# Block transposes that write with stride four, whole-tile loads and stores, and a new hand-written order in a hashed-attention and MLP kernel

## The chip, the cores and the metric

The kernel runs on one core of a Trainium2 chip. The metric is device time in microseconds (us) of one execution. Five engines work from queues of their own: PE (TensorE, matrix products), DVE (VectorE), ACT (ScalarE), POOL (GpSimd) and SP (SyncE, which here only issues transfers). An instruction starts when it is at the head of its engine's queue and what it waits for is there.

## The reference, cut to what matters

Attention in which a query sees only keys with the same six-bit hash, then a layer norm and a two-layer MLP with a residual.

```python
q_bits = (np.einsum('bhsd,dk->bhsk', q, proj) > 0)      # k_bits likewise; 6 bits
mask = q_bucket[:, :, :, None] == k_bucket[:, :, None, :]
scores = np.where(mask, scale * np.matmul(q, k.transpose(0, 1, 3, 2)), -1e9)
attn = softmax(scores); x = np.matmul(attn, v)           # 4 batches, 8 heads, 768 rows, 64 wide
x = x.transpose(0, 2, 1, 3).reshape(4, 768, 512)
xn = (x - mu) / np.sqrt(var + 1e-06) * g_ln
out = x + np.maximum(xn @ w_ch1, 0.0) @ w_ch2            # 512 -> 2048 -> 512
```

## The kernel before

The work is cut into 12 units u: batch b = u // 3 and a third of its 768 queries, 256 rows. A unit has six score steps s = 6u ... 6u+5, three key blocks of 256 for each of two groups g of four heads.

**A score step.** `S` is 24 matmuls (L476): hash signs from `G` and two halves of q and k, summed so that equal hashes lift a score. It writes two PSUM pairs, heads 0 and 1 into `sc(s, 0)`, heads 2 and 3 into `sc(s, 1)`. `E` (L482, ACT) takes the exponential of one pair, 128x1024, and frees it. `A` (L501) multiplies E by the values `vaug` into `acc`. The pairs have the tags scA and scB; only for the steps in `ROT = (2, 1, 0)`, the first three, a third pair, `acc`, takes part in turn.

**After three steps of a group:** `na`, `nb` normalize (L514, L521, L523), `nc` and `ce` are the statistics and centring (L527, L530, L531), `rs` is on POOL. `fl` transposes the result by a DMA into `xnT`; unit 0 does it by PE (`ft`, `fc`). `F.u.p` (L558, 8 matmuls) is the first MLP product for two of 16 hidden blocks, `R` its relu on DVE or ACT, `D` the second product (L574), `Z` the residual (L582), `O` the store (L592).

**The feed.** A tile `X` holds q or k as loaded, 32 sequence rows on the partitions of each head. DVE transposes 32x32 blocks (`turn`, L234): `tn` for batch 0 in pieces of one key block (`tp`, 128x256, two instructions per piece), `tu` for later batches (`T`, 128x384, eight per group). The sequence index is 32-row block, `c` (0..3) and `t` (0..31) mixed: a transpose writes contiguously, so that within each 128 columns the order is (c, t) and not the natural (t, c). Batch 0 puts its keys right in the casts and hash copies (`ca`, `bh`, `bi`, through `key_order`); later batches instead load the values in four 32-partition pieces (`lv`, L378), and every output is stored in four such pieces (L592). The hash signs come through `ha` (L323) and `bh`, or for the rest of batch 0 through `hc`, `bc`, `sl`, `bi` (L334 to L359), later through `hm`, `bt` and a DRAM round trip `mw`, `mr`. `cv` casts values on POOL, `su`, `sp`, `sq`, `sc` sum them. `lw1`, `lw2` are the weight loads, issued by POOL; `wm` and `warm` are matmuls on ones while the first loads are under way, and `wa`, the same into unused columns of `acc`, is defined but not in the order.

**What sets the order.** A list of words written into the source, each an operation, its engine (t PE, v DVE, a ACT, p POOL, s SP) and its arguments. The kernel issues them in that sequence, so each engine's queue order is the list's.

Of the kernel before, what the change touches and what calls it, by code (L numbers as in the profile page):

```python
# [13 lines left out]
NWARM = 8  # L14

ROT = (2, 1, 0)
# [3 lines left out]
on.p.0 mem.v lp.a tab.a warm.t wm.t.0 wm.t.1 lx.s.0.0.0.1 lx.s.0.1.1.3 pf.v wm.t.2 wm.t.3 lx.s.1.1.0.3 lx.s.0.1.0.1  # L20
lx.s.1.0.0.1 tn.v.0.0.0 ca.a.0.0.0 lx.s.1.0.1.3 lv.s.0.0.4 lv.s.0.4.4 sel.p lx.s.0.0.1.3 p32.p ha.t.0.0.0 wm.t.4 wm.t.5
tn.v.0.1.2 ca.a.0.1.2 bh.v.0.0.0 tn.v.0.1.1 ca.p.0.1.1 ha.t.0.1.2 ha.t.0.1.1 bh.v.0.1.2 S.t.2.2 tn.v.1.1.2 ca.p.1.1.2
wm.t.6 wm.t.7 E.a.2.0 E.a.2.1 lg.s tn.v.0.1.0 ha.t.0.1.0 bh.v.0.1.1 tn.v.1.0.0 S.t.1.2 E.a.1.0 ca.p.0.1.0 ca.p.1.0.0
bh.v.0.1.0 tn.v.1.1.1 ca.v.1.1.1 ha.t.1.1.1 cv.p.0.0.0 E.a.1.1 gx.p.1.0.0 LX.s.1.0.0 bh.v.1.1.1 cv.p.0.0.2 S.t.0.2
E.a.0.0 ha.t.1.0.0 tn.v.1.1.0 ha.t.1.1.0 bh.v.1.0.0 S.t.4.2 bh.v.1.1.0 E.a.0.1 ca.p.1.1.0 tn.v.1.0.2 ha.t.1.1.2
bh.v.1.1.2 cv.p.0.4.2 tn.v.0.0.2 lv.s.1.4.3 A.t.1.2 cv.p.0.4.0 E.a.4.0 sq.t.0.0 lw1.p.2 E.a.4.1 lv.s.1.0.3 S.t.3.2
A.t.2.2 lv.s.1.4.0 sc.a.0.0 lw1.p.1 E.a.3.0 tn.v.0.0.1 hc.t.0.0.2 hc.t.0.0.1 bc.v.0.0.1 E.a.3.1 bc.v.0.0.2 sl.t.0.0.1
bi.a.0.0.1 ca.v.0.0.1 tn.v.1.0.1 sl.t.0.0.2 S.t.5.2 ca.p.1.0.1 lv.s.1.4.1 bi.a.0.0.2 E.a.5.0 A.t.0.2 na.v.0.0 nb.v.0.0
nc.v.0.0 sq.t.0.4 E.a.5.1 sc.v.0.4 S.t.8.2 gx.v.1.0.1 E.a.8.0 gx.v.1.1.0 A.t.5.2 A.t.4.2 ca.p.1.0.2 tu.v.1.0.0.0
LX.s.1.0.1 A.t.3.2 E.a.8.1 na.v.0.1 nb.v.0.1 lw1.p.3 S.t.6.2 E.a.6.0 lv.s.1.0.1 nc.v.0.1 ce.v.0.0 hc.t.1.0.2 hc.t.1.0.1  # L30
A.t.8.2 bc.v.1.0.1 E.a.6.1 S.t.7.2 A.t.6.2 bc.v.1.0.2 lv.s.1.4.2 ce.v.0.1 E.a.7.0 pmem.p tu.v.1.0.0.1 rs.p.0 gx.v.1.1.1
sl.t.1.0.1 on.p.1 sl.t.1.0.2 LX.s.1.1.1 bi.v.1.0.2 bi.v.1.0.1 E.a.7.1 lw1.p.0 tu.v.1.0.0.3 ft.t.0.1 ft.t.0.0 fc.v.0.0
LX.s.1.1.0 S.t.9.2 tu.v.1.0.1.2 fc.a.0.1 A.t.7.2 lw2.p.1 lw2.p.0 tu.v.1.0.1.1 lw2.p.3 ca.a.0.0.2 cv.p.1.4.0 F.t.0.4
tu.v.1.0.1.3 E.a.9.0 E.a.9.1 na.v.1.0 F.t.0.3 R.v.0.4 S.t.10.2 R.a.0.3 A.t.9.2 lw2.p.2 E.a.10.1 F.t.0.6 tu.v.1.0.0.2
CA.v.1.0.0 E.a.10.0 nb.v.1.0 nc.v.1.0 R.a.0.6 F.t.0.7 S.t.11.2 E.a.11.0 tu.v.1.0.1.0 E.a.11.1 CA.p.1.0.1 su.p.1.4
hm.t.1.0 bt.v.1.0 A.t.10.2 R.a.0.7 tu.v.1.1.0.2 tu.v.1.1.1.3 tu.v.1.1.1.1 S.t.14.2 tu.v.1.1.0.1 mw.s.1.0 mr.s.1.0.0
F.t.0.2 tu.v.1.1.0.3 R.v.0.2 A.t.11.2 E.a.14.1 na.v.1.1 nb.v.1.1 E.a.14.0 F.t.0.5 tu.v.1.1.1.2 S.t.12.2 R.v.0.5 F.t.0.0
E.a.12.0 nc.v.1.1 R.v.0.0 E.a.12.1 A.t.14.2 F.t.0.1 S.t.13.2 A.t.12.2 R.a.0.1 lv.s.1.0.2 D.t.0.0.0 E.a.13.0 ce.v.1.0
E.a.13.1 D.t.0.0.1 ce.v.1.1 rs.p.1 fl.s.1.1 tu.v.1.1.1.0 fl.s.1.0 tu.v.1.1.0.0 mr.s.1.0.3 S.t.16.2 E.a.16.0 E.a.16.1
LX.s.2.0.0 mr.s.1.0.2 hm.t.1.1 lv.s.1.0.0 bt.v.1.1 CA.p.1.1.0 mr.s.1.0.1 D.t.0.0.2 mw.s.1.1 sp.t.1.4 sc.v.1.4 S.t.15.2  # L40
cv.p.1.4.2 F.t.1.7 R.v.1.7 E.a.15.0 E.a.15.1 cv.p.1.0.0 A.t.13.2 D.t.0.0.3 na.v.2.0 F.t.1.5 CA.a.1.1.1 Z.v.0.0 S.t.17.2
LX.s.2.1.1 E.a.17.1 R.v.1.5 mr.s.1.1.3 su.p.1.0 D.t.0.1.0 F.t.1.2 R.v.1.2 LX.s.2.0.1 mr.s.1.1.1 mr.s.1.1.0 LX.s.3.0.1
D.t.0.1.1 E.a.17.0 S.t.18.2 E.a.18.1 lv.s.2.0.3 mr.s.1.1.2 F.t.1.3 R.v.1.3 D.t.0.1.2 D.t.0.1.3 nb.v.2.0 E.a.18.0
F.t.1.0 lv.s.2.0.0 A.t.15.2 S.t.20.2 E.a.20.0 R.v.1.0 F.t.1.1 R.a.1.1 Z.v.0.1 tu.v.2.0.0.1 A.t.17.2 nc.v.2.0 A.t.16.2
F.t.1.4 cv.p.1.0.2 tu.v.2.0.0.3 E.a.20.1 S.t.19.2 E.a.19.0 na.v.2.1 A.t.20.2 R.v.1.4 nb.v.2.1 nc.v.2.1 ce.v.2.1
lv.s.2.4.1 tu.v.2.0.0.2 D.t.1.0.0 E.a.19.1 fl.s.2.1 F.t.1.6 R.a.1.6 S.t.21.2 D.t.1.0.1 E.a.21.0 E.a.21.1 lv.s.2.4.2
ce.v.2.0 tu.v.2.0.0.0 D.t.1.0.2 D.t.1.0.3 CA.p.2.0.0 tu.v.2.0.1.0 tu.v.2.0.1.1 sp.t.1.0 sc.a.1.0 A.t.18.2 fl.s.2.0
S.t.22.2 E.a.22.1 LX.s.2.1.0 E.a.22.0 tu.v.2.0.1.2 tu.v.2.0.1.3 CA.a.2.0.1 hm.t.2.0 O.s.0.0 lv.s.2.0.1 Z.v.1.0 bt.v.2.0
D.t.1.1.0 S.t.23.2 F.t.2.0 LX.s.3.0.0 E.a.23.1 D.t.1.1.1 lv.s.2.4.3 lv.s.2.4.0 R.a.2.0 E.a.23.0 tu.v.2.1.0.0 lv.s.2.0.2
A.t.19.2 na.v.3.0 F.t.2.5 R.a.2.5 cv.p.2.4.0 S.t.24.2 E.a.24.0 D.t.1.1.2 tu.v.2.1.1.2 F.t.2.3 su.p.2.0 E.a.24.1 R.v.2.3  # L50
rs.p.2 A.t.23.2 S.t.26.2 F.t.2.2 D.t.1.1.3 nb.v.3.0 tu.v.2.1.1.1 cv.p.2.0.0 E.a.26.1 E.a.26.0 R.v.2.2 A.t.21.2 F.t.2.1
R.a.2.1 O.s.0.3 tu.v.2.1.0.1 S.t.25.2 nc.v.3.0 Z.v.1.1 mw.s.2.0 E.a.25.0 O.s.0.2 O.s.1.3 E.a.25.1 A.t.22.2 na.v.3.1
nb.v.3.1 F.t.2.4 tu.v.2.1.1.0 O.s.0.1 mr.s.2.0.2 D.t.2.0.0 tu.v.2.1.1.3 R.a.2.4 S.t.29.2 sp.t.2.0 sc.v.2.0 A.t.25.2
E.a.29.0 A.t.26.2 tu.v.2.1.0.3 O.s.1.0 F.t.2.7 cv.p.2.0.2 nc.v.3.1 ce.v.3.1 E.a.29.1 R.a.2.7 S.t.28.2 A.t.24.2 F.t.2.6
E.a.28.0 lv.s.3.4.2 LX.s.3.1.0 E.a.28.1 cv.p.2.4.2 D.t.2.0.1 ce.v.3.0 R.a.2.6 tu.v.2.1.0.2 S.t.31.2 fl.s.3.1 E.a.31.0
fl.s.3.0 E.a.31.1 CA.p.2.1.1 hm.t.2.1 bt.v.2.1 tu.v.3.0.1.0 tu.v.3.0.1.2 mw.s.2.1 mr.s.2.1.0 mr.s.2.1.2 D.t.2.0.2
rs.p.3 tu.v.3.0.1.3 mr.s.2.1.3 S.t.27.2 su.p.2.4 E.a.27.0 D.t.2.0.3 na.v.4.0 F.t.3.7 A.t.28.2 R.v.3.7 E.a.27.1 S.t.30.2
E.a.30.0 lv.s.3.0.1 Z.v.2.0 A.t.27.2 nb.v.4.0 E.a.30.1 A.t.29.2 D.t.2.1.0 mr.s.2.0.3 F.t.3.1 nc.v.4.0 R.v.3.1 na.v.4.1
nb.v.4.1 O.s.1.2 S.t.32.2 E.a.32.0 CA.v.2.1.0 D.t.2.1.1 D.t.2.1.2 E.a.32.1 LX.s.3.1.1 F.t.3.6 R.a.3.6 lv.s.3.4.1
S.t.35.2 E.a.35.0 E.a.35.1 nc.v.4.1 D.t.2.1.3 F.t.3.4 R.v.3.4 Z.v.2.1 A.t.30.2 S.t.34.2 F.t.3.3 mr.s.2.0.1 O.s.1.1  # L60
A.t.31.2 ce.v.4.0 E.a.34.0 R.a.3.3 O.s.2.0 A.t.32.2 E.a.34.1 F.t.3.0 na.v.5.0 S.t.33.2 E.a.33.0 R.v.3.0 A.t.35.2
E.a.33.1 F.t.3.2 ce.v.4.1 O.s.2.1 mr.s.2.0.0 A.t.34.2 fl.s.4.1 D.t.3.0.0 fl.s.4.0 tu.v.3.0.0.2 R.v.3.2 lv.s.3.0.2
tu.v.3.0.1.1 on.p.2 rs.p.4 tu.v.3.0.0.0 S.t.37.2 F.t.3.5 CA.v.3.0.1 mr.s.2.1.1 R.v.3.5 D.t.3.0.1 E.a.37.1 tu.v.3.0.0.3
tu.v.3.0.0.1 E.a.37.0 CA.p.3.0.0 D.t.3.0.2 S.t.38.2 E.a.38.1 nb.v.5.0 E.a.38.0 sp.t.2.4 sc.v.2.4 D.t.3.0.3 hm.t.3.0
bt.v.3.0 S.t.36.2 mw.s.3.0 F.t.4.1 Z.v.3.0 E.a.36.0 R.v.4.1 tu.v.3.1.1.0 A.t.33.2 na.v.5.1 tu.v.3.1.0.3 D.t.3.1.0
O.s.2.2 lv.s.3.4.0 E.a.36.1 S.t.39.2 D.t.3.1.1 E.a.39.1 F.t.4.7 R.v.4.7 nb.v.5.1 mr.s.3.0.1 O.s.2.3 tu.v.3.1.0.2
nc.v.5.1 A.t.38.2 D.t.3.1.2 E.a.39.0 lv.s.3.0.0 F.t.4.0 R.v.4.0 tu.v.3.1.0.1 S.t.40.2 E.a.40.0 D.t.3.1.3 Z.v.3.1
# [41 lines left out]
def kernel(  # L109
# [527 lines left out]
```

## Time and profile before

| what | value |
|---|---|
| median of 3 runs | 308.56 us (307.54 to 309.51) |
| span of the profiled execution | 308.1 us |
| POOL, ACT and DVE busy | 84.6, 187.9 and 174.4 us |
| exponentials, 144 of 128x1024 | 153.5 us, 1110 ns each |
| transposes T, 48 of 128x384, and tp, 24 of 128x256 | 25.5 us, 558 ns each, and 9.1 us, 419 ns each |
| stores | 50 issues on SP, 6 on ACT |
| value loads | 26 issues on SP |
| weight loads, from issue to landing | 9.1 to 15.9 us, median 11.5 |

The span runs from the first instruction to the last. Busy time of an engine is no bound by itself: an engine that is always busy in a stretch sets that stretch's length, and a wait counts only there. A row of the costliest groups names line, engine, operation, tiles and shapes, then total busy time and the mean of one, then idle time before it and what ended that.

### The profile page before, as it was taken

Reading aid. Unit: us, or ns where it says so; the run is one execution under the profiler, and the core shown is the slowest. Engines: PE = TensorE matmul, PEld = TensorE weight load, DVE = VectorE, ACT = ScalarE, POOL = GpSimd, SP = SyncE. Lnnn points to the kernel's source line nnn. Section 1 sums busy time; section 2 is a strip of 40 time slices with the busy share of each in tenths; the row PEclk is TensorE's granted clock in tenths of the full one; section 3 lists DMA queues with packets and bytes.
Section 4 is the critical chain, followed back from the end, with each engine's and each line's share of the span. In section 5 each row is a group of like instructions: output and inputs, shape, how many; then the busy total and the mean of one; then the engine's idle time right before and its main releaser. Section 6 shows DMA issues by size and latency. Waiting matters only on the chain.

```text
span 308.1 us, 9875 instructions
## 1 busy us (share of the span) xinstructions
PE 297.0 (96%) x4394; PEld 203.9 (66%) x4394; DVE 174.4 (57%) x363; ACT 187.9 (61%) x204; POOL 84.6 (27%) x102
## 2 busy tenths in 40 slices
PE   8898699999999999999999999999999999999994
PEld 4576477567667766856676677676676776676663
DVE  4757777646926956666866434556464335345112
ACT  3687667775786867755657586665755686351220
POOL 3675625626233950141020028301001001001000
PEclk9999779999999999999999999999999999999999
DMA  6999999488594587124032030131010501103032
GB/s 213 358 263 194 296 252 199 69 248 232 118 278 112 135 106 192 46 65 129 2 87 54 9 108 2 40 81 36 10 45 19 102 4 27 43 2 91 30 85 69
DMA packets 31290, 34.32 MB, mean 111 GB/s; under 512 B 15632, under 2 KB 27920, under 8 KB 31248
## 3 DMA queue, kind: packets, MB, share of 16 engines
q1 hardware_dynamic: 26656, 29.24, 37.2%
q0 software_dynamic: 4224, 4.19, 8.4%
q8 instruction: 34, 0.56, 0.8%
q10 hardware_dynamic: 368, 0.26, 0.3%
q14 instruction: 8, 0.07, 0.1%
HBM read 28.12 MB, written 6.88 MB: 114 GB/s over the span
## 4 chain that ended last, share of the span: by engine, by line
PE 86%; DVE 4%; DMA 4%; ACT 3%; SPq 1%; issue 1%; DVEq 0%
PE f L558 27%; PE sc L476 17%; PE acc L501 11%; ACT E L482 3%; DMA X<-in_k_dram 3%; PE hp L431 2%; PE hf L323 1%; DMA xnT<-xc 1%; PE f_60None L574 1%; PE f_11None L574 1%; PE f_31None L574 1%; PE f_71None L574 1%; PE f_50None L574 1%; PE f_21None L574 1%; PE f_20None L574 1%; PE f_101None L574 1%
## 5 line engine op out<-in xcount | busy, mean ns | idle before, releaser
L482 ACT ACTIVATE E<-sc,bias_sb 128x1024 bf16<-128x1024 f32 x144 | 153.5, 1110 | 64.1 <-PE sc L476 64.1
L558 PE MATMUL f<-xnT,w_sb 128*128 128x256 bf16 x768 | 100.6, 275 | 0.2 <-DMA xnT<-xc 0.2
L558 PEld LDWEIGHTS <-w_sb 128*128 128x128 bf16 x768 | 71.9, 98 | 22.1 <-issue 5.2
L568 DVE TENSOR_SCALAR hb<-f 128x512 bf16<-128x512 f32 x48 | 33.0, 688 | 46.9 <-PE f L558 46.3
L574 PEld LDWEIGHTS <-hb 128*128 128x128 bf16 x400 | 36.7, 98 | 33.3 <-issue 4.5
L476 PE MATMUL sc<-qb,kb 32*128 32x256 bf16 x1152 | 53.1, 269 | 0.0
L566 ACT ACTIVATE hb<-f 128x512 bf16<-128x512 f32 x48 | 28.6, 596 | 39.9 <-PE f L558 38.5
L501 PEld LDWEIGHTS <-E 128*128 128x128 bf16 x1152 | 41.8, 98 | 7.4 <-issue 5.1
L501 PE MATMUL acc<-vaug,E 128*128 128x65 bf16 x1152 | 45.7, 195 | 0.0
L476 PE MATMUL sc<-G 6*128 6x256 bf16 (+1 forms) x576 | 43.3, 275 | 1.8 <-ACT E L482 1.7
L536 POOL TENSOR_SCALAR rs<-mv 128x2 f32<-128x2 f32 x12 | 7.8, 654 | 123.2 <-DVE mv L530 122.9
L476 PEld LDWEIGHTS <-kb 32*128 32x128 bf16 x1152 | 30.8, 94 | 1.6
L476 PEld LDWEIGHTS <-G 6*128 6x128 bf16 (+1 forms) x576 | 16.1, 91 | 20.6 <-issue 18.7
L234 DVE STREAM_TRANSPOSE T<-X 128x384 f32<-128x384 f32 x48 | 25.5, 558 | 3.7 <-DMA X<-in_q_dram 3.7
L514 DVE SCALAR_TENSOR_TENSOR y<-vsB,acc 128x520 f32<-128x520 f32 x24 | 16.5, 687 | 18.0 <-PE acc L501 18.0
L531 DVE SCALAR_TENSOR_TENSOR xc<-x,mv,gB 128x512 bf16<-128x512 f32 x24 | 19.1, 798 | 0.9
L381 POOL CAST vaug<-vn 128x768 bf16<-128x768 f32 x16 | 13.5, 859 | 17.8 <-DMA vn<-in_v_dram 11.8
L527 DVE BATCH_NORM_STATS2 st<-x 128x6 f32<-128x256 f32 x48 | 17.6, 411 | 0.3
L389 POOL TENSOR_TENSOR t<-vn 128x768 f32<-128x768 f32 x6 | 10.9, 1814 | 24.7 <-DMA vn<-in_v_dram 24.7
L523 DVE TENSOR_TENSOR x<-y,rc 128x512 f32<-128x512 f32 x24 | 17.2, 715 | 0.8
L243 POOL TENSOR_SCALAR qb<-T 128x1536 bf16<-128x1536 f32 x3 | 12.8, 4267 | 13.5 <-DVE T L234 8.7
L234 DVE STREAM_TRANSPOSE tp<-X 128x256 f32<-128x256 f32 x24 | 9.1, 419 | 3.9 <-DMA X<-in_k_dram 2.8
(115 smaller groups left out, 240.1 us busy)
## 6 DMA issues: line engine op xcount, KB each, us to landing
out_dram<-x SPq DMA_DIRECT2D x44, 128.0 KB
X<-in_k_dram SPq DMA_DIRECT2D x7, 768.0 KB
X<-in_q_dram SPq DMA_DIRECT2D x6, 768.0 KB
vn<-in_v_dram SPq DMA_DIRECT2D x24, 192.0 KB
w_sb<-in_moe_w_ch_dram POOLq DMA_DIRECT2D x8, 512.0 KB, 11.5
vn<-in_v_dram SPq DMA_DIRECT2D x2, 768.0 KB
X<-in_q_dram SPq DMA_DIRECT2D x2, 512.0 KB
Bd<-B SPq DMA_DIRECT2D x6, 96.0 KB
```

Of the source, the lines that this page charges most:

```text
L234: nc.vector.transpose(d[:, j], s[:, j, kj0 : kj0 + n])
L476: nc.tensor.matmul(sc(s, i // 2)[:, i % 2, 256 * kk : 256 * kk + 256], lh, rh, start=(rep == 0), stop=(rep == 2), skip_group_check=True,)
L482: nc.scalar.activation(E(s)[:, heads(h)], sc(s, h), AF.Exp, scale=EXP_SCALE, bias=bias_sb)
L501: nc.tensor.matmul(acc[:, qt, (D + 1) * i : (D + 1) * (i + 1)], E(s)[:, i, 256 * kk + P * qt : 256 * kk + P * qt + P], vaug(u // 3)[:, 4 * ...
L514: nc.vector.scalar_tensor_tensor(yt(u, g), vs, EPS_ROW, made[f"acc{u}{g}"][:, :, :A], op0=AOP.mult, op1=AOP.add,)
L523: nc.vector.tensor_tensor(xo, a[:, :, :, 0:D], rc.to_broadcast([P, 2, 4, D]), op=AOP.mult)
L527: nc.vector.bn_stats(stats(u)[:, qt, g], xt(u)[:, qt, 256 * g : 256 * g + 256])
L531: nc.vector.scalar_tensor_tensor(xc(u)[:, t], xt(u)[:, t], mv(u)[:, t, 0:1], gB, op0=AOP.subtract, op1=AOP.mult,)
L558: nc.tensor.matmul(f1[:, n].rearrange("p (t x) -> p t x", t=2), w1_sb[:, dt, P * nt : P * nt + P], xnT(u)[:, :, dt], start=(dt == 0), stop ...
L566: nc.scalar.activation(hb(u)[:, 2 * p : 2 * p + 2], f1, AF.Relu)
L568: eng.tensor_scalar_max(hb(u)[:, 2 * p : 2 * p + 2], f1, 0.0)
L574: nc.tensor.matmul(f2, hb(u)[:, nt, P * t : P * t + P], w2_sb[:, nt, half(h)], start=(nt == 0), stop=(nt == NNT - 1),)
```

## The change

Transposes write each block with a stride of four elements, so that q, k and T are in natural order. `key_order` goes; values load in one transfer per four heads (8 for 26), outputs store in one per unit (14 issues for 56, three of them for unit 11). Six score steps rotate over three pairs, the third made of the two single banks f1 and f2, whose exponentials are taken in halves. `acc` is two single banks instead of one pair of banks, and `na` works on each of them. The hash tiles `hf` move to the acc banks but for four of them. `cv` may run on any engine, `ag` is split from `ce`, `wa` is used four times, `warm` is one matmul and not eight. The order is written anew. Its part up to the first `F` and the edits (repeats of the same kind left out):

```diff
-NWARM = 8
-ROT = (2, 1, 0)
+NWARM = 1
+ROT = (2, 1, 0, 4, 3, 5)
...
+lx.s.0.1.1.2 mem.v lp.a lx.s.0.0.0.1 wm.t.1 lx.s.0.1.2.3 wm.t.5 wm.t.7 lx.s.0.1.0.1 wm.t.3 lx.s.1.0.0.1 wm.t.4 wm.t.6
+lx.s.1.1.0.3 pf.v wm.t.2 lv.s.0.0 warm.t tn.v.0.1.1 lx.s.0.0.1.3 wm.t.0 ca.p.0.1.1 ha.t.0.1.1 tn.v.0.0.0 lv.s.0.4
+sel.p ha.t.0.0.0 tn.v.0.1.2 bh.v.0.1.1 ca.a.0.1.2 ca.v.0.0.0 ha.t.0.1.2 bh.v.0.0.0 tn.v.0.1.0 S.t.1.2 tn.v.1.0.0
+gx.p.1.0.1 ca.a.0.1.0 LX.s.1.0.1 ha.t.0.1.0 E.a.1.1 bh.v.0.1.2 lx.s.1.0.1.3 ca.p.1.0.0 ha.t.1.0.0 bh.v.0.1.0 E.a.1.0
+tn.v.1.1.1 S.t.2.2 bh.v.1.0.0 ca.p.1.1.1 tn.v.1.1.0 ha.t.1.1.1 E.a.2.1 cv.p.0.0.0 ha.t.1.1.0 E.a.2.0 bh.v.1.1.1 p32.p
+tn.v.1.1.2 S.t.0.2 cv.p.0.0.2 bh.v.1.1.0 tn.v.0.0.1 ha.t.1.1.2 E.a.0.0 lv.s.1.0 ca.v.1.1.2 lg.s ca.v.0.0.1 sq.t.0.0
+E.a.0.1 bh.v.1.1.2 cv.p.0.4.0 S.t.4.2 sc.a.0.0 ca.p.1.1.0 hc.t.0.0.1 E.a.4.0 on.p.0 bc.v.0.0.1 sl.t.0.0.1 A.t.1.2
+bi.v.0.0.1 E.a.4.1 tn.v.0.0.2 S.t.3.2 cv.v.0.4.2 gx.p.1.0.0 lw1.p.1 A.t.2.2 LX.s.1.0.0 E.a.3.0 tu.v.1.0.1.2 lv.s.1.4
+A.t.0.2 na.v.0.0 E.a.3.1 S.t.5.2 nb.v.0.0 A.t.4.2 E.a.5.0 su.p.1.0 A.t.3.2 tn.v.1.0.1 E.a.5.1 nc.v.0.0 S.t.8.2 E.a.8.0
+hc.t.1.0.1 sq.t.0.4 bc.v.1.0.1 tn.v.1.0.2 E.a.8.1 sl.t.1.0.1 A.t.5.2 sc.v.0.4 lw1.p.3 sp.t.1.0 na.v.0.1 bi.a.1.0.1
+S.t.6.2 lw1.p.0 sc.a.1.0 nb.v.0.1 hc.t.0.0.2 pmem.p E.a.6.1 wa.t.1.0.1 ca.p.1.0.1 nc.v.0.1 wa.t.1.0.3 E.a.6.0
+wa.t.1.0.2 ag.v.0.0 ag.v.0.1 ce.v.0.1 wa.t.1.0.0 bc.v.0.0.2 S.t.7.2 ce.v.0.0 lw1.p.2 sl.t.0.0.2 tu.v.1.0.0.2 E.a.7.1
+ft.t.0.1 on.p.1 A.t.6.2 su.p.1.4 bi.v.0.0.2 A.t.8.2 fc.v.0.1 E.a.7.0 tu.v.1.0.0.0 hc.t.1.0.2 ca.v.1.0.2 ft.t.0.0
+bc.v.1.0.2 fc.a.0.0 S.t.9.2 sl.t.1.0.2 E.a.9.1 A.t.7.2 bi.v.1.0.2 F.t.0.2 tu.v.1.0.1.1 gx.p.1.1.1 lw2.p.0 LX.s.1.1.1
...
-    v_view = [v[b].rearrange("h (tt c kj) d -> c tt h (kj d)", tt=TT, c=CC) for b in range(B)]
-    out_view = [out[b].rearrange("(tt c u qt) d -> u c tt qt d", tt=TT, c=CC, u=3) for b in range(B)]
+    v_view = [v[b].rearrange("h (p kj) d -> p h (kj d)", p=P) for b in range(B)]
+    out_view = [out[b].rearrange("(p u qt) d -> u p (qt d)", p=P, u=3) for b in range(B)]
...
     def turn(dst, src, j, kj0, n):
         s = src.rearrange("p (c kj j dd) -> p j kj c dd", c=CC, j=2, dd=32)
-        d = dst.rearrange("p j (kj c t) -> p j kj c t", c=CC, t=32)
+        d = dst.rearrange("p j (kj t c) -> p j kj c t", c=CC, t=32)
...
     def hf(g, t, kp):
-        return ps(f"hf{g}{t}{kp}", [P, 512], ("f1", "f2")[(t + kp + g) % 2])
+        return ps(f"hf{g}{t}{kp}", [P, 512], "acc" if t or not kp else ("f1", "f2")[g])
...
     def sc(s, h):
-        tag = ("scA", "scB", "acc")[(2 * ROT.index(s) + h) % 3] if s in ROT else ("scA", "scB")[h]
-        return ps(f"sc{s}{h}", [P, 2, 512], tag)
+        pair = (2 * ROT.index(s) + h) % 3 if s in ROT else h
+        if pair == 2:
+            return [ps(f"sc{s}.{h}.{n}", [P, 512], ("f1", "f2")[n]) for n in range(2)]
...
     def na(eng, u, g):
+        for qt in range(2):
+            nc.vector.scalar_tensor_tensor(
+                yt(u, g)[:, qt], vs, EPS_ROW, made[f"acc{u}{g}{qt}"][:, :A], op0=AOP.mult, op1=AOP.add,
+            )
```

## The prediction

> **What bounds the kernel now.** I read the page's busy times first, then the busy time by stretch, then the chain of waits, then the rows by shape.
>
> ```profile
> PE 297.0 (96%) x4394; PEld 203.9 (66%) x4394; DVE 174.4 (57%) x363; ACT 187.9 (61%) x204; POOL 84.6 (27%) x102
> ```
>
> PE is nearly always busy. The busy time by stretch (start:end, length, busy us and instructions of PE, PEld, DVE, ACT, POOL, granted clock, DMA share, GB/s) says where it is not:
>
> ```profile
> 27.00:30.00 3.00, 2.68 (x78) 2.21 (x72) 2.31 (x9) 2.12 (x2) 0.98 (x3) 1.00 1.03 149
> 30.00:33.00 3.00, 2.28 (x78) 1.74 (x72) 2.90 (x9) 2.12 (x2) 0.38 (x1) 1.00 1.14 296
> 33.00:36.00 3.00, 1.29 (x30) 0.95 (x24) 1.09 (x4) 2.12 (x2) 2.92 (x7) 0.83 1.09 262
> 36.00:40.00 4.00, 3.79 (x51) 2.85 (x52) 3.12 (x8) 2.44 (x4) 2.79 (x4) 0.50 1.01 345
> 200.00:250.00 50.00, 49.99 (x760) 35.15 (x753) 25.15 (x48) 30.95 (x34) 2.98 (x4) 1.00 0.22 46
> ```
>
> From about 40 us on PE has no idle time, so the rest is PE's work at its rate. The opening, and the clock that falls to 0.50 after the hole at 33 to 36, is where time can be had. The chain of waits (start, length, what) shows the opening's pace:
>
> ```profile
> 21.19 2.13 ACT E L482 x2
> 23.32 0.04 issue
> 23.36 0.75 PE sc L476 x20
> 24.11 0.02 issue
> 24.14 2.13 ACT E L482 x2
> 26.26 0.04 issue
> 26.30 0.84 PE sc L476 x22
> 27.15 2.12 ACT E L482 x2
> ...
> 33.79 1.39 issue
> 35.19 0.52 PE hf L347 x6
> ...
> 39.63 2.88 PE f L558 x16
> 42.52 0.77 PE sc L476 x24
> 43.28 0.60 PE acc L501 x16
> 43.88 1.75 PE f L558 x16
> ```
>
> With two pairs, S waits for both exponentials of the step before, and the next exponential for S: a step takes 2.13 + 0.84 = 3.0 us. At 13.19, where the third pair takes part, the timeline has four exponentials back to back in 4.20 us: 2.1 a step. The same 16 matmuls of F take 2.88 us at the low clock and 1.75 after it: 1.1 us lost.
>
> **The method.** The list up to the first F (before F.0.4 at 39.45) has ten S and nine A in both kernels, and what is left, 96 F, 62 S, 63 A, 100 D and 6 hm, is the same work with 289 changes of kind between neighbours before and 284 after; five sp matmuls are left where six were. So the new time follows from when the first F (now F.0.2) starts, plus what changes behind it.
>
> **The opening, walked through with rows of before.** Loads: 256 KB had landed at 4.14 and 768 KB by 6.33, so the new sequence of 256 KB pieces lands at about 4.1, 5.2 and 6.3, then, at the 330 GB/s of 6 to 9 us, the 768 KB of group 1's keys at 10.3 and its values by 12.7 and 16.5. A pair of transposes takes 0.77 us (timeline, 4.14), taken here as unchanged; a DVE hash copy 0.42, a cast 0.42 (the contiguous row).
> - DVE: three pairs as they land, to 7.1, then bh, ca, bh to 8.4. S.1 runs 8.5 to 9.4. ACT has ca.a.0.1.0 ahead of the first E: its transposes end at 9.15, 0.63 for a contiguous cast, so E starts at 9.8, as before (9.80).
> - S.2 waits for the hash copy at 10.3 and scA at 10.9; E 12.0 to 14.1 (before 13.19). S.0 waits for ha.1.1.0, whose transposes end at 12.7: E 14.1 to 16.3 (15.3).
> - S.4 waits behind sq for cv on POOL, queued after casts of 1.99 and 1.07 us, 15.4, and sq takes 0.83: E.4 starts at 17.0 (17.96).
> - A.1 waits for on.p.0, behind the second value load (16.5), cv 0.83, a cast 1.07 and on 0.55: 18.9. A takes 0.65, S 0.84: E.3 20.3 (21.19).
> - Now the rotation works: S.5 finds scB and f1, f2 free, E.5 22.6 (24.14); E.8 24.8 (27.14).
> - Steps 8, 6, 7, 9 have two pairs again, 3.0 us each: E.6 27.8 (30.14), E.7 30.8 (33.09). Group 1's A.5 ends near 25.5; na, nb, nc, ag, ce follow on DVE (0.83, 0.9, 0.75, 0.4, twice 0.75) to 30.4; ft and fc between A.6, A.8 and S.9; A.7 ends at 34.9. First F: 35.0 (39.45).
>
> Term 1: **-4.4 us**. 1.0 of it is there at E.4 (smaller first loads, shorter casts), 1.4 comes from E.4 to E.8 (the rotation), 2.1 after it, mostly the wait for sl and bi at 33.79 to 36.2, which has no place here: S.9 stands ahead of sl.1.0.2, and the copies bi run beside it.
>
> Term 2, the clock: between 24 and 33 us PE was busy 2.28 to 2.68 of each 3 us and kept 1.00; the fall followed the hole. My walk has no hole over 1.3 us, so the 1.1 us go: **-1.1** (nothing, if a hole comes; +2 if it is longer).
>
> **The other edits.**
> - na: 687 ns for 128x520; with 412 for 128x256 from PSUM, 2 x 0.41 = 0.83. That is 24 x 0.14 = 3.4 us of DVE, beside matmuls: DVE is busy 25.15 of 50 us at 200 to 250. Uncovered it would cost up to 3.4.
> - Half exponentials: 596 ns (the relu row, same size) twice against 1110, four times: 0.3 us on ACT, in steps whose gaps hold it.
> - cv: eight of 16 leave POOL, four each for DVE and ACT, where 128x768 takes about 0.8 us (1024 take 1.11). An E or a relu behind one starts that much later; PE has products of the other kinds queued between. Uncovered: 3.2.
> - wa: eight matmuls, about 0.1 us each, in PE's waits for E. One warm-up matmul for eight: nine in all at 0.43 us (8 in 3.45) end at 5.0, when the first hash product can start; nothing.
> - 60 fewer issues at 0.32 to 0.42 us leave SP. Its longest waits are for DVE's xc and x, so nothing gained; O now waits for both halves of Z and stands ahead of LX and fl on SP, but comes right behind its Z in the list. su on POOL waits for V and holds lw1 behind it (a rival, below).
> - Tail: the last Z ended at 304.25, the end came 3.85 us later. One store of 128 KB for four of 32 KB over two queues saves a second issue of 0.4 and may land later: -0.8 to +0.5, taken **-0.2**.
> - Relus and Z behind a new list: PE idled 0.2 us behind 39.45; I allow **+0.5** (0 to 3).
>
> Sum: 308.1 - 4.4 - 1.1 - 0.2 + 0.5 = 302.9, and with the median 0.46 above the span **303.3**. Chance 0.48; its own range 300.5 to 305.5.
>
> **Rival 1, slower: the strided write.** No row has a write with a stride of four fp32. Nearest rows, all strided reads (128 bytes) of the same 128x512: ACT 1116 ns against 631 contiguous, 0.95 ns more per element; POOL 1074 for 512 against 1692 for 1536, about double per element; DVE 652 against 419, which may be the loss of a two-at-a-time mode. From PSUM DVE paid nothing (412 strided, 464 not). So a transpose costs between nothing more and 0.95 ns per element: 419 to 663, 558 to 923. I take nothing, since these are reads and this is one write per cycle on the engine that showed least; the upper end is the rival. The Trainium skill, SBUF — State Buffer, section Door 1: The DMA port swizzle, speaks against the change: consecutive accesses keep full rate only with two hits in a 16-byte line, and a stride of four fp32 gives one; yet it names four fp32 as free, so it can be read both ways. The reads in the trace agree with the first reading; no row of it shows the write. By the first reading the sum would be rival 1's, by the second the forecast's.
> At the upper end DVE gets 24 x 0.24 + 48 x 0.36 = 23 us more. In the opening, three pairs ahead of S.1 (1.0 late after load waits), six ahead of S.0 (2.5), eight ahead of S.4 (3.5): first F at 38.5, 0.9 saved for 4.4. Behind it, six bursts of eight T's each put 2.9 us in front of relus that free the single bank f1: 17 us if all is met by PE, nothing if none; in 50 to 55 DVE is busy 4.93 of 5. With a third, 6: 308.56 - 0.9 - 1.1 - 0.2 + 6 = 312.4, from 306 to 319. It decides once a 384-element transpose passes about 0.7 us. Chance 0.34.
>
> **Rival 2, same: the transfers set the pace.** DMA is full (share 1.0 or more) from 3 to 50 us. Order puts su.p.1.0, which needs a whole 768 KB of V, ahead of lw1.3, lw1.0, lw1.2 on POOL, and sp.1.0 ahead of S.6 on PE. My walk has V at 23, su 1.81 + 0.73 + 0.73 to 26.3, lw1.0 issued at 27.9, landing 9.1 to 15.9 later: 37 to 43.8, and F.0.0 is due at 39. Before, a V piece issued at 28.5 landed at 38.58. For it: those 10 us. Against: whole tiles, fewer packets. It gives back 2 to 5 us: 305.5 to 308.5, about 307. Chance 0.18.
>
> **How the numbers follow.** 1% is about what a measurement of this kernel tells from none: 305.5 and 311.6. Faster: 0.44 from the forecast, 0.03 from each rival, 0.50. Slower: 0.23 from rival 1, 0.04 from rival 2, 0.01: 0.28. The rest 0.22. The range runs from 300.5, the forecast's lower end, to 313.5, which leaves out the worse part of rival 1, some 0.13.
>
> **What would show it.** The rows of L240 (the new transposes): 558 and 419 ns right, above 700 for T rival 1. First F near 35 with E steps 2.1 us apart for s = 0, 4, 3, 5. PEclk at 1.00 through 30 to 45; a second fall would undo term 2. PE idle before L389 (sp) or L562 (F), released by POOL or a DMA, is rival 2. PE idle between 40 and 300 released by DVE or ACT relus would be the lists' fault or the transposes'. If first F is at 35 and the time is not near 303, the equality of the work behind it was the wrong step.

## The result and the profile after

The changed kernel takes 322.77 us (median, 321.07 to 324.37) where the kernel before took 308.05 beside it: ratio 1.047, 95% interval 1.041 to 1.053. It is slower; 303.3 had been forecast, and the time lies outside the range of 300.5 to 313.5. One execution of a_swap (371.5 us) and one of d_fix2_rot3 (1634.1 us) ran in a slower state; the medians below leave them out, and no row of these two traces is used.

The profiled execution has a span of 319.6 us (before 308.1), and it splits at two points that the prediction used:

| stretch | before | after | difference |
|---|---|---|---|
| start to first F | 39.45 | 35.37 | -4.1 |
| first F to the end of the last Z | 264.8 | 281.6 | +16.8 |
| last Z to the end | 3.85 | 2.62 | -1.2 |

So the opening came out as forecast (35.0), and the loss is all behind it. The spans differ by 11.5 us and the medians by 14.7: on record a time is 1.7 above its own span, so before's profiled execution took about 309.8, 1.8 above its median, and after's took 321.35, 1.4 below its own. The page's busy times, after:

```profile
PE 295.6 (92%) x4350; PEld 205.6 (64%) x4395; DVE 197.5 (62%) x389; ACT 191.4 (60%) x214; POOL 72.3 (23%) x94
```

PE is 1.4 us less busy in a span 11.5 us longer: it waits. (After's trace has 4350 matmuls for 4395 weight loads, before's 4394 for 4394, so some matmul records are missing and PE was busier than the page says.) DVE has 23 us more. The busy time by stretch says where (columns as in the prediction):

```profile
60.00:70.00 10.00, 7.11 (x122) 5.28 (x114) 7.44 (x8) 4.15 (x6) 3.15 (x1) 0.83 0.30 100
100.00:110.00 10.00, 9.84 (x156) 7.25 (x158) 9.63 (x15) 8.66 (x10) 2.49 (x1) 1.00 0.15 52
110.00:120.00 10.00, 4.58 (x34) 1.78 (x34) 9.93 (x16) 3.38 (x5) 6.17 (x6) 0.77 0.47 162
120.00:140.00 20.00, 19.89 (x317) 13.41 (x318) 12.40 (x25) 12.08 (x12) 0.00 (x0) 0.94 0.37 113
```

Two holes, at 60 to 70 and 110 to 120, and each takes the granted clock down with it, the second to 0.50 at 116 to 120 and 0.89 at 120 to 130; it is back at 1.00 from 130 on. In the second DVE is busy 9.93 of 10 us with only 16 instructions, where before it did 15 in 7.20. Before, those stretches had 9.83 and 10.00 of PE at clock 1.00. PE's waits behind the first F, from its timeline: 0.72, 1.37, 0.68, 2.84, 5.37, 1.26 and 0.54, together 12.8 us, against 0.2 before. The two longest in the timeline (start, length, engine, line, operation, tiles; in brackets the idle time ahead of it and what ended it):

```profile
59.06 4.08 POOL L249 TENSOR_SCALAR qb<-T 128x1536 bf16<-128x1536 f32 x1 [11.11 <-DVE T L240]
...
59.73 4.23 DVE L251 CAST kb<-T 128x1536 bf16<-128x1536 f32 x1
...
63.89 0.54 DVE L243 TENSOR_SCALAR B<-hp 128x384 bf16<-128x384 f32 x1
...
64.48 0.80 PE L562 MATMUL f<-xnT,w_sb 128*128 128x256 bf16 x3 [2.84 <-DVE B L243]
...
107.51 4.10 POOL L249 TENSOR_SCALAR qb<-T 128x1536 bf16<-128x1536 f32 x1 [29.05 <-DVE T L240]
...
108.01 3.27 DVE L525 TENSOR_TENSOR x<-y,rc 128x512 f32<-128x512 f32 x1
...
111.58 1.80 POOL L382 TENSOR_TENSOR t<-vn 128x768 f32<-128x768 f32 x1
111.91 2.90 DVE L377 CAST vaug<-vn 128x768 bf16<-128x768 f32 x2
...
115.39 0.67 DVE L572 TENSOR_SCALAR hb<-f 128x512 bf16<-128x512 f32 x1
...
116.11 0.39 PE L389 MATMUL vp<-vsum,ones 128*128 128x256 bf16 x1 [5.37 <-DVE hb L572]
```

The row of this k cast on DVE before (L245) and after (L251; busy us, mean ns of one):

```profile
L245 DVE CAST kb<-T 128x1536 bf16<-128x1536 f32 x2 | 1.9, 940 | 0.0
L251 DVE CAST kb<-T 128x1536 bf16<-128x1536 f32 x3 | 7.4, 2483 | 0.0
```

The k cast at 59.73 takes 4.23 us; the same cast takes 0.94 where POOL is idle. POOL's scaling of q beside it ends at 63.14, and 0.82 later, a little less than its own length, the cast is done: it stood until POOL was finished. `B` and with it the bank f1 come 3.3 us late, and F waits. At 108.01 a multiplication that takes 0.69 elsewhere takes 3.27 beside the next scaling; two value casts then take 2.90 together beside POOL's sums (0.55 each at their shortest); the relu is behind all of them on DVE, and `sp` (L389) needs the bank that this relu frees.

Before had scalings of q on POOL just as long, at 58, 83 and 135 us. Its timeline around the first and the last, with all that DVE started while the first ran:

```profile
58.12 4.11 POOL L243 TENSOR_SCALAR qb<-T 128x1536 bf16<-128x1536 f32 x1
60.48 0.56 DVE L237 TENSOR_SCALAR B<-hp 128x384 bf16<-128x384 f32 x1 [2.45 <-PE hp L431]
61.53 0.42 DVE L411 COPY vsB<-vp 128x256 f32<-128x256 f32 x1 [0.49 <-PE vp L396]
...
135.48 0.69 DVE L523 TENSOR_TENSOR x<-y,rc 128x512 f32<-128x512 f32 x1
...
135.52 4.61 POOL L243 TENSOR_SCALAR qb<-T 128x1536 bf16<-128x1536 f32 x1 [4.68 <-DVE rc L521]
```

Beside the first, DVE works from PSUM (`hp`, `vp`) at its usual pace. At 135.48 DVE's multiplication was there first, and POOL's scaling took 0.5 longer. So whoever starts second waits, and the old list had put nothing on DVE there that has to wait. The Trainium skill, SBUF — State Buffer, section Who interferes with whom, describes just this: DVE and GpSimd share one pair of SBUF ports, which a DVE cast or scaling in its fast mode, or an operation with two SBUF inputs against a GpSimd one that reads SBUF, must have to itself for the whole instruction, and the later one blocks. These rows agree with it, the transposes too: at 82.27 five of them took 2.41 us in all, 0.5 each, while POOL's second scaling ran from 83.03; only the multiplication at 108.01 ended 0.3 ahead of POOL's end.

The transposes' own rows in after's groups (busy, mean ns, idle before):

```profile
L240 DVE STREAM_TRANSPOSE T<-X 128x384 f32<-128x384 f32 x48 | 38.4, 859 | 0.7 <-DMA X<-in_q_dram 0.7
L240 DVE STREAM_TRANSPOSE tp<-X 128x256 f32<-128x256 f32 x24 | 12.8, 625 | 2.0 <-DMA X<-in_k_dram 2.0
```

859 for 558 and 625 for 419, 0.78 and 0.80 ns more per element, 17 us of DVE in the two rows' busy time. Two theories went to the chip. **Theory 1:** the strided write, by this DVE time, costs the 14.7 us. **Theory 2:** the new list's pairing of DVE's SBUF operations with POOL's long ones does.

### The profile page after: what moved, and what is told of

The parts are those of the page before. It is cut to its first block, busy times and chain, and to the rows that moved or that the text cites. A ratio compares the mean times of both kernels' runs of the same rounds, so it can differ in the third digit from the quotient of the medians.

```text
span 319.6 us, 9799 instructions
## 1 busy us (share of the span) xinstructions
PE 295.6 (92%) x4350; PEld 205.6 (64%) x4395; DVE 197.5 (62%) x389; ACT 191.4 (60%) x214; POOL 72.3 (23%) x94
## 4 chain that ended last, share of the span: by engine, by line
PE 75%; DVE 16%; DMA 5%; issue 2%; ACT 1%; SPq 1%; DVEq 0%
PE f L562 24%; PE sc L472 13%; PE acc L502 8%; DVE T L240 4%; DMA X<-in_q_dram 2%; DVE x L525 2%; PE hf L322 2%; PE hp L424 2%; DMA vn<-in_v_dram 2%; DMA X<-in_k_dram 2%; PE f_20None L578 2%; DVE hb L572 2%; DVE kb L251 1%; DVE y L516 1%; DVE st L529 1%
## 5 line engine op out<-in xcount | busy, mean ns | idle before, releaser
L480 ACT ACTIVATE E<-sc,bias_sb 128x1024 bf16<-128x1024 f32 x140 | 149.7, 1111 | 63.1 <-PE sc L472 60.4
L572 DVE TENSOR_SCALAR hb<-f 128x512 bf16<-128x512 f32 x46 | 31.6, 688 | 58.2 <-PE f L562 57.4
L472 PE MATMUL sc<-G 6*128 6x256 bf16 (+1 forms) x560 | 41.9, 274 | 1.8 <-ACT E L480 1.7
L240 DVE STREAM_TRANSPOSE T<-X 128x384 f32<-128x384 f32 x48 | 38.4, 859 | 0.7 <-DMA X<-in_q_dram 0.7
L540 POOL TENSOR_SCALAR rs<-mv 128x2 f32<-128x2 f32 x12 | 3.9, 323 | 98.1 <-DVE x L586 74.7
L516 DVE SCALAR_TENSOR_TENSOR y<-vsB,acc 128x260 f32<-128x260 f32 x48 | 18.1, 418 | 6.3 <-PE acc L502 6.2
L525 DVE TENSOR_TENSOR x<-y,rc 128x512 f32<-128x512 f32 x24 | 19.7, 823 | 0.9
L535 DVE SCALAR_TENSOR_TENSOR xc<-x,mv,gB 128x512 bf16<-128x512 f32 x24 | 17.7, 741 | 0.4
L377 POOL CAST vaug<-vn 128x768 bf16<-128x768 f32 x8 | 7.7, 975 | 33.8 <-PE sc L472 27.0
L382 POOL TENSOR_TENSOR t<-vn 128x768 f32<-128x768 f32 x6 | 11.8, 1964 | 11.6 <-DMA vn<-in_v_dram 11.5
L240 DVE STREAM_TRANSPOSE tp<-X 128x256 f32<-128x256 f32 x24 | 12.8, 625 | 2.0 <-DMA X<-in_k_dram 2.0
```

Of the source, the lines that this page charges most:

```text
L240: nc.vector.transpose(d[:, j], s[:, j, kj0 : kj0 + n])
L472: nc.tensor.matmul(sc(s, i // 2)[i % 2][:, 256 * kk : 256 * kk + 256], lh, rh, start=(rep == 0), stop=(rep == 2), skip_group_check=True,)
L480: nc.scalar.activation(E(s)[:, 2 * h : 2 * h + 2], whole, AF.Exp, scale=EXP_SCALE, bias=bias_sb)
L516: nc.vector.scalar_tensor_tensor(yt(u, g)[:, qt], vs, EPS_ROW, made[f"acc{u}{g}{qt}"][:, :A], op0=AOP.mult, op1=AOP.add,)
L525: nc.vector.tensor_tensor(xo, a[:, :, :, 0:D], rc.to_broadcast([P, 2, 4, D]), op=AOP.mult)
L535: nc.vector.scalar_tensor_tensor(xc(u)[:, t], xt(u)[:, t], mv(u)[:, t, 0:1], gB, op0=AOP.subtract, op1=AOP.mult,)
```

## The experiments

Times are medians; "before" in the same runs was 307.6 to 308.2. First F and last Z are from each profiled execution.

### One cause at a time

**a_contig**: the changed kernel, but transposes write contiguously as before. Rows of q and k then stand in another order than values and results, so the output differs; the work is the same.

```diff
-        d = dst.rearrange("p j (kj t c) -> p j kj c t", c=CC, t=32)
+        d = dst.rearrange("p j (kj c t) -> p j kj c t", c=CC, t=32)
```

> The changed kernel with contiguous transpose writes; everything else, the order too, as changed (rows and values are then paired in different orders, so the attention of batch rows is a different computation of the same cost). Theory 1, the strided write costs the time: T falls from 860 to about 560 ns and tp from 622 to about 410, PE's idle time behind the first F shrinks from about 13 us to 4 or less, time 308 or less, first F 1 to 3 us earlier. Theory 2, POOL's scaling of q beside DVE's casts and normalisation costs it: the casts of 4.2 and 2.3 us and the product of 3.3 us stay, time 314 or more.

Measured 316.94 (ratio 1.029, 1.023 to 1.034). T is back at 554 ns; the k casts beside POOL still take 2.4 and 4.5 us, and `sp` still waits 4.3 for a relu. 5.8 of 14.7 us.

**a_qact**: the three scalings of q go from POOL to ACT (1.48 us there).

```diff
-CA.p.1.0.0   CA.p.1.1.0   CA.p.2.1.0
+CA.a.1.0.0   CA.a.1.1.0   CA.a.2.1.0
```

> The changed kernel with the three scalings of q (CA.p.1.0.0, CA.p.1.1.0, CA.p.2.1.0) on ACT instead of POOL. Theory 2: the DVE casts of k beside them fall from 2.3 and 4.2 us to about 0.94, the product x from 3.3 to 0.69; the PE waits at 45, 61 and 111 us go, about 8 us: time 312 to 315. Theory 1: no more than 3 us are gained, 319 to 322, since DVE is still late.

Measured 314.72 (1.020, 1.013 to 1.026). The transposes are as slow as in the changed kernel (859 ns), but the k casts take 905 to 961 ns, the longest L525 is 1.25 us instead of 3.27, and the clock is 1.00 throughout. 8.0 of 14.7 us, by three words of the list.

**b_stride4**: the kernel before with the strided write and, since the order is now natural, without `key_order`; values and results keep their pieces.

```diff
-        d = dst.rearrange("p j (kj c t) -> p j kj c t", c=CC, t=32)
+        d = dst.rearrange("p j (kj t c) -> p j kj c t", c=CC, t=32)
...
-v_view = ... "h (tt c kj) d -> c tt h (kj d)"     out_view = ... "(tt c u qt) d -> u c tt qt d"
+v_view = ... "h (c tt kj) d -> c tt h (kj d)"     out_view = ... "(c tt u qt) d -> u c tt qt d"
```

> The kernel before with stride-four transposes and natural order in q, k and v (no reordering in the casts of batch 0; loads and stores still in four pieces); same list. Theory 1: T at 860 ns and tp at 622 in the old list too, DVE about 19 us busier, first F later by 1 to 4 us, time 312 to 318. Theory 2: the longer transposes alone are covered, 307 to 310.

Measured 309.64 (1.005, 1.002 to 1.008), with T at 864 ns and DVE 13.5 us busier: in the old list the slow transposes, less whatever the dropped reordering saves (no run holds the two apart), cost 1.5 us. PE's waits for DVE behind its first F are 1.9 us in all. Theory 1 falls as the cause of the whole; the price seems to depend on the list, 1.5 us net in one and 5.8 in the other.

**b_collide**: the opposite test. In the kernel before, only two k casts go from ACT to DVE, beside scalings that POOL had all along; one of them also moves up in the list, to its scaling.

```diff
-CA.p.1.1.0 ... CA.a.1.1.1 ...               CA.a.2.0.1
+CA.p.1.1.0 CA.v.1.1.1 ...                   CA.v.2.0.1
```

> The kernel before, with only two k casts of 1536 elements moved from ACT to DVE, so that they stand beside POOL's q scalings at 58 and 83 us; POOL's scalings stay where they were. Theory 2: these casts last 2.5 to 4.2 us instead of 0.94, DVE's relus and B behind them come late, 310 to 314 us. Rival (what counts in the changed kernel is that q comes late from POOL, not DVE's lengthened operations): casts near 0.95 us, or long but hidden, 307.5 to 309.5, the time of before.

Measured 310.00 (1.0085, 1.0047 to 1.0123), at the edge of theory 2's interval and above the rival's. Its timeline, of an execution of 312.64, the longest of ten:

```profile
60.53 2.10 DVE L247 CAST kb<-T 128x1536 bf16<-128x1536 f32 x1
...
63.00 1.03 PE L560 MATMUL f<-xnT,w_sb 128*128 128x256 bf16 x8 [1.17 <-DVE vsB L413]
...
83.60 4.09 POOL L245 TENSOR_SCALAR qb<-T 128x1536 bf16<-128x1536 f32 x1 [11.68 <-DVE T L236]
...
85.29 3.21 DVE L247 CAST kb<-T 128x1536 bf16<-128x1536 f32 x1
88.42 0.73 DVE L584 SCALAR_TENSOR_TENSOR x<-f_10None,rs,x 128x512 f32<-128x512 f32 x1
89.08 0.54 DVE L239 TENSOR_SCALAR B<-hp 128x384 bf16<-128x384 f32 x1
89.21 1.02 PE L576 MATMUL f_11None<-w_sb,hb 128*128 128x512 bf16 x4 [1.65 <-DVE x L584]
```

The cast at 85.29 ends 0.81 us behind POOL's scaling (83.60 + 4.09 = 87.69; 85.29 + 3.21 = 88.50). PE's idle time at 60 to 100 rises from 0.17 to 2.82 us, and the time by 2.3. POOL's scaling was neither moved nor later: DVE's stretched operations are what costs, 5.3 us for the two casts where their own length is 1.9; what 1.9 us more on DVE would have cost by themselves, no run shows.

### Is the rest the sum of both?

**a_contig_qact_cva**: contiguous writes, q scalings on ACT, and the three value casts that DVE has at 112 and 180 on ACT as well (`cv.v.2.0.0`, `2.0.2`, `3.0.2` to `cv.a`). Rows are paired as in a_contig.

> Contiguous transpose writes (rows and values then paired in different orders, same cost), the three scalings of q on ACT, and three value casts (cv.v.2.0.0, cv.v.2.0.2, cv.v.3.0.2) on ACT instead of DVE. Both theories together: first F near 34 us, little PE idle time behind it, time 301 to 305, that is the prediction's walk with its assumption restored. If 308 or more, something else in the list or the transfers keeps PE waiting.

Measured 309.19 (1.003, 1.000 to 1.006), and not 301 to 305. PE now waits 3.5 us for exponentials (0.7 of it was there in the changed kernel) and 1.3 for relus on ACT. The longest wait, 1.45 at 107.3, has four casts on ACT ahead of it between 101.8 and 107.5: work taken off DVE blocked another queue.

**a_swap** and **a_contig_swap** therefore exchange letters: q scalings go to DVE (0.9 to 1.3 us in a_contig_swap and c_swap_fix), the k casts to POOL (1.5 to 2.1).

```diff
-CA.p.1.0.0 CA.v.1.0.1   CA.p.1.1.0 CA.v.1.1.1   CA.p.2.1.0
+CA.v.1.0.0 CA.p.1.0.1   CA.v.1.1.0 CA.p.1.1.1   CA.v.2.1.0
```

> The changed kernel with letters exchanged: POOL's three q scalings of 1536 elements (4.1 us each) go to DVE (0.95 us each by the other q rows), and the two k casts that DVE did beside them go to POOL (1.5 us by its k cast row). Theory 2 (a DVE operation from SBUF to SBUF that meets POOL's scaling lasts until the scaling ends): L525's longest under 1.3 us, 313 to 316 us, as with the scalings on ACT (314.7). If the 4.4 us that ACT got there were part of what was left, 311 to 313 here. If only the late arrival of q counted and not DVE's longer operations: 314 to 316 as well, so this run does not tell that apart; b_collide does.

> Both at once: contiguous writes of the transposes (the rows then stand in another order, so scores and values are paired wrongly) and the exchanged letters. If the two costs add (5.8 and 8.0 us): 308 to 310. If the waits that ACT's extra work made in the run with both on ACT (309.2, S and F waiting for ACT in 36 to 50 and 100 to 120) were real costs: 305 to 308.

Measured 313.09 (1.017, 1.009 to 1.025) and, with contiguous writes, 308.20 (1.003, 0.999 to 1.007). The first is at the lower edge of the interval for no gain over ACT, and a_qact is within its uncertainty, so ACT's 4.4 us of extra work is not shown to have cost much there. The second is where adding the two costs puts it. The strided write is worth 4.9 us in this list too.

### The other parts of the change

**a_stride2**: the changed kernel with a stride of two elements, 8 bytes, instead of four; rows are paired wrongly again.

```diff
-        d = dst.rearrange("p j (kj t c) -> p j kj c t", c=CC, t=32)
+        d = dst.rearrange("p j (kj c2 t c1) -> p j kj c2 c1 t", c1=2, c2=2, t=32)
```

> The changed kernel with the transposes writing at a stride of two fp32 (8 bytes) instead of four (rows are then paired wrongly). If the cost needs a stride of 16 bytes: T 558 and tp 419 ns, and about 317 us as with contiguous writes. If it begins with any stride: T near 860.

One execution, 315.71 us. The rows:

```profile
L240 DVE STREAM_TRANSPOSE T<-X 128x384 f32<-128x384 f32 x48 | 25.3, 556 | 0.0
L240 DVE STREAM_TRANSPOSE tp<-X 128x256 f32<-128x256 f32 x24 | 9.1, 420 | 2.4 <-DMA X<-in_k_dram 2.2 <-DMA X<-in_q_dram 0.3
```

A stride of 8 bytes costs nothing, one of 16 costs half as much again. Of the two readings of the Trainium skill's SBUF — State Buffer, section Door 1: The DMA port swizzle, that the prediction weighed, the one by which two accesses must fall in a 16-byte line agrees with these rows, and the one by which four fp32 are free does not. Strides between and beyond were not tried.

**a_swap_pieces**: a_swap with the data layout of before: contiguous writes, key reordering in batch 0, values of batches 1 to 3 in four loads and every result in four stores, all on SP.

> The changed kernel with the exchanged letters and the data layout of before: contiguous writes, keys reordered in the casts of the first batch, values of the later batches in four loads, results in four stores. Beside a_contig_swap (308.2) it differs in that reordering and in the split transfers alone. If the whole-tile transfers were worth something: 309.5 to 312. If not: 307.5 to 309.5. If the strided write explains what is left of a_swap (313.5): 5 us under that.

Measured 318.76 (1.037, 1.032 to 1.041), 10.6 us more than a_contig_swap, against an expectation of 4 at most. Of the 11.1 us between the two spans 4.0 lie ahead of the first F (38.56 against 34.52), 3.0 in the stretch behind it, 4.1 in the tail, where its four stores are on one queue while before used two. In the opening POOL's sums stand 5.0 and 1.7 us for value loads (2.1 and nothing in a_contig_swap) and hold back weight loads behind them, and `sp` waits 2.9 us for a sum. So in this list the layout of before costs more than the whole-tile one. Which share is the reordering's and which the split loads', these runs do not separate.

**a_rot3**: the changed kernel with `ROT = (2, 1, 0)`.

> The changed kernel with three score steps over the three pairs instead of six, nothing else. If the rotation gives what the walk said, steps 4, 3 and 5 come 3.0 us apart again: first F 1.0 to 1.8 us later (36.4 to 37.2), time 323.5 to 325. If the opening was set by loads and hashes instead: first F within 0.4 of 35.4 and the time within 1 of 322.8.

Measured 321.69 (1.044, 1.038 to 1.050), no slower than the changed kernel, though its first F came at 37.99, 2.6 us later: neither interval was met. Of the 2.6 us, 2.1 stand at step 8's exponential; behind it two multiplications (L535) took 1.25 and 1.08 beside POOL's sums, 0.75 and 0.74 in the changed kernel. Part of the giving back can be read: in the changed kernel the first k cast starts at 44.18, meets POOL's scaling (41.57 to 45.67) and takes 2.31 us; with three steps the cast starts at 46.8, behind the scaling, and takes 1.20. At the third scaling the lead is 1.8 us (107.51 against 109.33), and 0.3 at the last Z.

### A list mended

**c_swap_fix**: a_swap, the three value casts of DVE on POOL, and the load `lv.s.3.0` moved up to `lv.s.3.4`.

```diff
-cv.v.2.0.0   cv.v.2.0.2   cv.v.3.0.2   lv.s.3.4 ... lv.s.3.0
+cv.p.2.0.0   cv.p.2.0.2   cv.p.3.0.2   lv.s.3.4 lv.s.3.0 ...
```

> The changed kernel (strided write, whole-tile transfers) with the exchanged letters, the three value casts of DVE on POOL and one value load issued earlier, for the holes at 100 to 120 and 160 to 200. Those holes were 2.7 us in a_contig_swap: 310.5 to 312.5. If the DVE time of the strided write is what is left, not these holes: 313 to 314.

Measured 309.72 (1.006, 1.003 to 1.009), 3.4 us under a_swap and better than expected. PE has no wait behind 120 any more. The longest that is left, in its timeline:

```profile
49.46 0.86 DVE L240 STREAM_TRANSPOSE T<-X 128x384 f32<-128x384 f32 x1 [2.82 <-DMA X<-in_q_dram]
50.17 0.67 DVE L572 TENSOR_SCALAR hb<-f 128x512 bf16<-128x512 f32 x1
...
50.89 1.38 PE L562 MATMUL f<-xnT,w_sb 128*128 128x256 bf16 x8 [2.22 <-DVE hb L572]
```

A transpose stands at the head of DVE's queue for its load, with a relu behind it and PE behind that.

**c_pieces_fix**: the same two edits on a_swap_pieces.

> The same two edits of the list on a_swap_pieces. If the holes are worth their length: 305 to 307, faster than before. If what is left behind the first F is spread over the whole span: 307.5 to 309.

Measured 314.86 (1.025, 1.020 to 1.030): 3.9 us gained here too, but from 318.8, so neither interval was met; the layout of before does not suit this list.

**d_fix2** puts that transpose, another and a scaling behind the relus they had held up; **d_fix2_rot3** adds the old rotation.

```diff
-tu.v.1.1.0.0 ... R.v.0.7        CA.v.2.1.0 ... tu.v.2.1.1.0 ... R.v.2.6
+R.v.0.7 tu.v.1.1.0.0            R.v.2.6 CA.v.2.1.0 tu.v.2.1.1.0
```

> c_swap_fix with two transposes and one q scaling queued on DVE behind the relu that PE waited for (2.2 us at 49, where the transpose stood for its load, and 1.1 us at 109). If the forecast's first term holds once the waits are gone (first F 35.2, equal work behind it, clock 1.00): 304 to 307, faster than before. If other waits take their place: 308 to 310, the time of c_swap_fix.

> The same with three score steps over the three pairs: first F 2.6 us later, as a_rot3's. If the opening's time reaches the end: 2 to 3 us above d_fix2. If it is given back at 40 to 60 (loads and DVE set the pace there): within 0.7 of d_fix2.

Measured 309.03 (1.003, 1.000 to 1.005) and 309.75 (1.006, 1.004 to 1.009). The two waits are gone and the clock is 1.00, but in its profiled execution the first F came at 37.20, with 1.6 us of PE's wait ahead of it for a copy on DVE. That copy stood behind a two-input multiplication (L536) of 2.16 us beside POOL's first value sum; in c_swap_fix, with the same order up to there, it started ahead of the sum and took 0.74. So the same collision can reach the opening too. The time hardly moved from c_swap_fix: d_fix2's first interval is missed, its second holds. The rotation is worth 0.7 us here, of a_rot3's 2.6, at the edge of the second interval. No version tried beats the kernel before; this one, which is the changed kernel but for eleven words of the order, comes within 0.3%.

## Why the prediction was wrong

**Term 1, -4.4 us: right.** First F at 35.37 for 35.0, a gain of 4.1. E starts at 10.75, 13.36, 16.04 and 18.53 us for steps 1, 2, 0 and 4, 1.0 to 1.9 later than in the walk; with contiguous writes (a_contig_swap) they start at 10.09, 12.78, 15.45 and 17.95, so the slower transposes explain at most 0.7 of that. Step 3 at 20.91 (20.3 in the walk) and step 8 at 25.20 (24.8) have made most of it up, and the copies `sl` and `bi` hold nobody. A hit within 0.4 us is partly luck, then, and d_fix2, with the same order up to its first F, shows 37.20. The rotation does what the walk said: with three steps instead of six, step 8 starts at 27.28, 2.1 later.

**"Transposes ... taken here as unchanged" and "takes nothing": wrong.** Reads did not tell of writes: 0.78 to 0.80 ns more per element, where ACT's strided read had 0.95. Rival 1's rows were right (558 to 923 held 859) and its price behind the first F, 6 us, nearly: 4.9 and 5.8 measured in this list. Its first F at 38.5 was wrong. With the scalings moved and the stride kept, a_swap took 313.1 for the 312.4 it gave, partly by chance, since 3.4 of that went with the value casts. But it could not make 322.8, and in the old list it came to 1.5 net.

**"Relus and Z behind a new list ... I allow +0.5 (0 to 3)": the step that failed.** PE's waits behind the first F were 12.8 us. The statement under it, that the work behind was the same with as many changes of kind and so took the same time, compares PE's work alone; what changed is which operations of DVE stand beside which of POOL. Three words of the list were worth 8.0 us (a_qact), the same pairing put into the old list 2.3 for two casts (b_collide). The page of before carried the warning unread: q scalings of 4.1 us on POOL, and k casts that were on ACT or POOL, or on DVE away from them. The prediction's last sentence had named this step as the one to doubt if first F was at 35 and the time not near 303, and so it was.

**cv, "Uncovered: 3.2": taken at nothing.** Moving three of DVE's four back to POOL, with one load issued earlier, gave 3.4 us (c_swap_fix against a_swap); the two edits were not tried apart. "A relu behind one starts that much later" was the mechanism, and 5.37 us of wait had two of them in it.

**Term 2, -1.1, the clock: right where it looked.** 30 to 60 us stayed at 1.00 (0.89 before). The fall came later, behind new holes: by estimate from the windows above 7.11 x 0.17, 4.58 x 0.23 and 19.89 x 0.06 us, together 3.5.

**Tail, -0.2:** -1.2. **na:** 418 ns for the 412 assumed. **Rival 2:** no wait behind the changed kernel's first F ended with a weight load (one of 1.2 us did in a_stride2), and the transfers were no worse; whole tiles helped, by up to the 10.6 us of a_swap_pieces, which the prediction had at next to nothing.

The sum of the profiled execution: -4.1 in the opening, +12.6 of waits, +2.4 of clock (3.5 for 1.1), -1.2 in the tail make 9.7 of the 11.5 us. The other 1.8 us, in the stretch behind the first F, are in no named hole; with matmul records missing, the small gaps there cannot be told from missing rows.

**"The median 0.46 above the span": mis-sized.** It set the median beside the span of another execution. On record each time is 1.7 above its own span, so the sum would have ended at 304.6 for an execution like the profiled one. Before's executions differ: those recorded beside the runs with a mean granted clock of 0.997 or more have spans of 303.6 to 305.7, those at 0.988 or 0.989 spans of 306.9 to 308.8, and the profiled one, at 308.1 and 0.989, is of the long kind. The median had less to gain from terms 1 and 2 than that trace shows; how much less, no trace tells.

**What stays open.** Why a mended list keeps only 0.7 of the rotation's 2.6 us: a_rot3 shows 1.1 of it, in a list with collisions; no line shows the rest. No run has contiguous writes, moved scalings and moved value casts at once with whole-tile transfers; if the three prices add, 322.8 - 4.9 - 9.7 - 3.4 gives an estimate of 304.8. The new places of `hf` and `acc` were not tried alone. Also open are the shares of reordering and split loads, and whether a list made for the strided write could be faster than before.

## What to carry to other kernels

Before saying that the work behind a point is the same, check for every long POOL operation what the new order puts on DVE beside it: here casts and two-input multiplications from SBUF to SBUF then lasted until POOL's operation was over, or nearly, while operations from PSUM, block transposes and a reciprocal (0.18 us at 107.79) took their usual time. The cost of a slower instruction belongs to the queue it stands in: 300 ns more per transpose cost 1.5 us net in the old list and about 5 where relus stood behind it. An earlier start counts only as far as it reaches the end; a run that undoes it alone tells.

## What the runs showed of the hardware that was not expected

- A 128x1536 cast on DVE takes 0.94 us alone and 2.1 to 4.5 beside POOL's 4.1 us scaling, ending 0.8 after it in the rows above (the two-input multiplication at 108.01 ended 0.3 ahead of POOL's end); POOL's scaling in turn took 4.61 where DVE's two-input multiplication had started 0.04 earlier.
- A DVE block transpose of fp32 writes at full rate with a stride of 8 bytes (556 ns for 128x384) and takes 1.54 times as long at 16 bytes (859).
- The granted clock was 0.77 over the ten us that held a wait of 5.37, 0.50 over 116 to 120, behind that wait, and 0.89 over the next ten. It fell to 0.83 in the ten us behind c_swap_fix's wait of 2.22 at 49, and stayed at 1.00 in a_qact, which had one of 2.21 at 50.99: the length of one wait does not decide it.
